# One fused attention and gating block on one core: start-up loads moved between two queues, idle matmuls added, a transpose issued a slot later, a last addition joined

## The chip, the core and the metric

The kernel runs on one core of a Trainium2 chip. The core has a matrix engine (TensorE, PE in the profile, with PEld for its weight loads), a vector engine (VectorE, DVE), an engine for functions (ScalarE, ACT), a general one (GpSimd, POOL) and an engine that here only issues transfers (SyncE, SP). Each has its own instruction queue, which it works through in order; they meet through semaphores. Transfers run on 16 DMA engines and are issued from SP's queue or from ACT's. The matrix engine writes to PSUM, in which this kernel keeps two double banks for scores (s_ps), two banks o_ps and two banks misc.

The metric is the device time of one execution in microseconds (us), less is better. The kernel before takes 1305.17 us, the median of three runs (1304.81 to 1305.69).

## The reference

```python
mod = (_silu(c) @ w_mod).reshape(c.shape[0], 6, 1, -1)
sa, ca, ga, sb, cb, gb = ...            # six rows of 512
h = _layernorm(x) * (1 + ca) + sa
x = x + ga * _A_ref(h, k_cache, v_cache, wq, wo)     # attention
h = _layernorm(x) * (1 + cb) + sb
x = x + gb * _B_ref(h, w_in, w_sp, b_sp, w_out)      # gated block
```

x has 2048 rows of 512. The attention has 32 query heads of 128, 8 heads of k and v with 2048 cached rows each, four query heads to one of k and v, softmax without a mask. The gated block projects to 2 x 896, applies gelu, normalises the second half, multiplies it along the rows with a 2048 x 2048 matrix w_sp, adds a bias, multiplies with the first half and projects back to 512. Everything comes and goes as bfloat16; sums are float32.

## The kernel before

**Units and iterations.** Rows are worked in 16 tiles of 128 (index j). A unit u is one group of four heads on one tile: 8 x 16 = 128 units, u = 16 g + j. One iteration `it` of the main loop issues the scores and exps of unit `it` in eight slots, and between them, by tables of functions to call at (iteration, slot), all the other work: the product with v of an earlier unit (`pv`), the output projection of a still earlier one (`wo_proj`), the query projection of a later group (`set_fill`), loads and norms. The order of every engine's queue is the order in which this Python code issues instructions; nothing reorders it.

**Rows and columns.** Of three successive units two are "by rows": their scores have query rows on partitions, the exps go to a row buffer, and each of the four heads is turned by a DMA transpose (pT) that SP issues (`turn_rows`), at slots 2, 4, 6 and at slot 0 of the next iteration. Their product with v comes two or three iterations later. The third unit, and all from unit 122 on, are computed already turned.

**Start.** At the start `c_bf` is loaded on ACT's queue, and on SP's queue x's first tile, two pieces of the modulation weights `wmod_a` (768 and 256 KB), half of k for group 0, weights of the first queries, and so on (L701 to L763). DVE casts c (L772), takes statistics of x's first tile (L697, L698); POOL makes the reciprocal root (L678, L682); DVE normalises (L686); ACT and DVE make silu(c). PE meanwhile runs `warm(10)`, idle matmuls on zeros (L777), then transposes x's tile (L897), multiplies the modulation weights with silu(c) (`mod_first`, L866), transposes part of k (`k_turn`, L856), runs two more idle matmuls, and projects the first queries (`first_q`, L927). DVE's copy to `modc` (L904) and the modulated tile `hT` (L805, L911) stand between `mod_first` and `first_q`. The first scores are L1040, their exps L1047.

**Second norm.** When the last group's output projection of tile j is done (in iteration `it`), `ln2` puts three steps into the table: `first` (statistics, reciprocal root) at slot 2 or 0 of the next iteration, `second` (normalisation to xn, and the DMA transpose xnT on SP's queue, L1207) at slot 4, and `third` (modulation of the turned tile into hT on DVE, L1214) at slot 3 of the iteration after. This happens from iteration 117 on. Iterations 117, 119 and 120 are units by rows, so that there SP also issues transposes of heads at even slots.

**Tail.** The gated block follows. For the last row tile the two halves of the final projection are multiplied with gb_rows by DVE (L1661), then x is added, one half by POOL and the other by DVE (L1665), and ACT's queue writes the tile (L1671).

Of the kernel before, what the change touches and what calls it, by code (L numbers as in the profile page):

```python
# [10 lines left out]
BF16 = mybir.dt.bfloat16  # L11
FP32 = mybir.dt.float32
ACT = mybir.ActivationFunctionType
ALU = mybir.AluOpType
AX = mybir.AxisListType
P = 128
# [559 lines left out]
def kernel(  # L576
# [19 lines left out]
    nc = tc.nc  # L596
    _, S, D = A_x.shape
    _, HKV, SK, DH = A_k_cache.shape
    HQ = A_wq.shape[1] // DH
    REP = HQ // HKV  # L600
# [5 lines left out]
    NDT = D // P  # L606
# [19 lines left out]
    wmod_dram = w_mod.rearrange("(p dt) n -> p dt n", p=P)  # L626
    c_dram = c[0].rearrange("(p j) -> p j", p=P)
# [18 lines left out]
    x_sb = res.tile([P, NT, D], BF16, name="x_sb")  # L646
# [10 lines left out]
    wmod_a = res.tile([P, NDT, 2 * D], BF16, name="wmod_a")  # L657
# [11 lines left out]
    def bank(name):  # L669
        return psum.tile([P, 512], FP32, name=name)  # L670
# [4 lines left out]
    def rstd_of(mv, n, tag):  # L675

        ve = stat.tile([P, CT], FP32, name=f"ve_{tag}")
        nc.gpsimd.tensor_scalar(  # L678
            out=ve[:, :n], in0=mv[:, :, 1], scalar1=LN_EPS, scalar2=None, op0=ALU.add
        )  # L680
        rstd = stat.tile([P, CT], FP32, name=f"rstd_{tag}", bufs=4)
        nc.gpsimd.tensor_tensor(out=rstd[:, :n], in0=ve[:, :n], in1=mhalf[:, :n], op=ALU.pow)  # L682
        return rstd

    def normalise(dst, src, mv, rstd):
        nc.vector.tensor_scalar(  # L686
            out=dst,
            in0=src,
            scalar1=mv,
            scalar2=rstd,  # L690
            op0=ALU.subtract,
            op1=ALU.mult,
        )

    def ln_stats(mv, j, src):
        st = stat.tile([P, 1, nc.vector.BN_STATS_DIM], FP32, name="bnst")
        nc.vector.bn_stats(out=st[:, 0, :], in_=src)  # L697
        nc.vector.bn_aggr(out=mv[:, j, :], in_=st[:])  # L698


    c_bf = res.tile([P, NDT], BF16, name="c_bf")  # L701
    nc.scalar.dma_start(out=c_bf[:], in_=c_dram)
    nc.sync.dma_start(out=x_sb[:, 0, :], in_=x_dram[:, 0, :])
    for kts in (slice(0, NDT - 1), slice(NDT - 1, NDT)):
        nc.sync.dma_start(out=wmod_a[:, kts, :], in_=wmod_dram[:, kts, 0 : 2 * D])
    k_nat = early.tile([P, SK], BF16, name="kT")

    def load_k_nat(half):
# [58 lines left out]
    zeros = late.tile([P, REP, DH], BF16, name="onorm", bufs=3)  # L767
# [2 lines left out]
    nc.gpsimd.memset(mean_bf[:], 1.0 / P)  # L770
    c_f = res.tile([P, NDT], FP32, name="c_f")
    nc.vector.tensor_copy(out=c_f[:], in_=c_bf[:])  # L772
    def warm(n):

        w_ps = bank("o_ps")
        for k in range(n):
            nc.tensor.matmul(  # L777
                w_ps[:].rearrange("p (r d) -> p r d", r=REP),
                lhsT=zeros[:, 0, :],
                rhs=zeros[:],  # L780
                start=True,
                stop=True,
            )
# [80 lines left out]
    def mod_first(kt, mc_ps):  # L864
        for col in range(2 * NDT):
            nc.tensor.matmul(  # L866
                mc_ps[:, col : col + 1],
                lhsT=wmod_a[:, kt, col * P : (col + 1) * P],
                rhs=sc_bf[:, kt : kt + 1],
                start=(kt == 0 and col == 0),  # L870
                stop=(kt == NDT - 1 and col == 2 * NDT - 1),
            )
        if kt == 0:
            nc.tensor.matmul(
                mc_ps[:, NDT : 2 * NDT],
                lhsT=mean_bf[:],
                rhs=ones_bf[:, 0:NDT],
                start=False,
                stop=False,
            )  # L880
# [10 lines left out]
    nc.vector.tensor_copy(out=sc_bf[:], in_=sc[:])  # L891
    xns0 = ln1_norm(0, 1, rstd0)
    mc_ps = bank("misc")
    warm(10)
    x_ps = bank("misc")[:].bitcast(BF16)[:, 0:D]
    for dt in range(NDT):
        nc.tensor.transpose(  # L897
# [1 line left out]
        )  # L899
    xT0 = res.tile([P, D], BF16, name="xn1", bufs=4)  # L900
    nc.vector.tensor_copy(out=xT0[:], in_=x_ps)
    for kt in range(NDT):
        mod_first(kt, mc_ps)
    nc.vector.tensor_copy(out=modc[:, 0 : 2 * NDT], in_=mc_ps[:, 0 : 2 * NDT])  # L904
    k_copy = k_turn((0, 1, 2, 3))
    warm(2)
    hT_of(0)
    for dt in range(NDT):
        dst, src = hTs[0][:, dt, 0:P], xT0[:, dt * P : (dt + 1) * P]
        if dt == 1:  # L910
            nc.scalar.activation(  # L911
                out=dst,
                in_=src,
# [87 lines left out]
    def at(it, slot, fn):  # L1001
        later.setdefault((it, slot), []).append(fn)
# [191 lines left out]
    def ln2(it, j):  # L1194

        st = {}

        def first():
            if j < NT - CT:
                ln_stats(mv2, j, x_sb[:, j, :])  # L1200
            st["rstd"] = rstd_of(mv2[:, j : j + 1, :], 1, "ln2")

        def second():
            xn = res.tile([P, D], BF16, name="xn2", bufs=2)
            normalise(xn[:], x_sb[:, j, :], mv2[:, j, 0:1], st["rstd"][:, 0:1])
            st["xnT"] = res.tile([P, NDT, P], BF16, name="xnT2", bufs=2)
            nc.sync.dma_start_transpose(out=st["xnT"][:], in_=xn[:])  # L1207

        def third():
            ch, c0 = j // CT, (j % CT) * P  # L1210
            if ch not in h2Ts:
                h2Ts[ch] = res.tile([P, NDT, 512], BF16, name="hT", bufs=NCH)
            for dt in range(NDT):
                nc.vector.tensor_scalar(  # L1214
                    out=h2Ts[ch][:, dt, c0 : c0 + P],
                    in0=st["xnT"][:, dt, :],
                    scalar1=modc[:, 4 * NDT + dt : 4 * NDT + dt + 1],
                    scalar2=modc[:, 3 * NDT + dt : 3 * NDT + dt + 1],
                    op0=ALU.mult,
                    op1=ALU.add,  # L1220
                )

        at(it + 1, 0 if j >= NT - CT else 2, first)
        at(it + 1, 4, second)
        at(it + 2, 3, third)

    mod_b = {}
# [120 lines left out]
    for g in range(1, HKV):  # L1348
        it = (g - 1) * NT
# [106 lines left out]
    for it in range(NU + 6):  # L1456
# [10 lines left out]
        for i in range(NSLOT):  # L1467
# [14 lines left out]
            elif pvs:  # L1482
                n = NSLOT // 2
# [10 lines left out]
        for u in wos:  # L1494
            if u >= (HKV - 1) * NT:
                ln2(it, u % NT)
        if it == NU + 2:
            free_b.close()
            mlp = fast.enter_context(tc.tile_pool(name="mlp", bufs=1, side="right"))
# [16 lines left out]
    for f in range(NFT):  # L1516
# [6 lines left out]
        out=ok1[:], in0=rall[:], scalar1=1.0 / SAFE, scalar2=None, op0=ALU.is_ge  # L1523
# [8 lines left out]
        out=bad[:], in0=okm[:], scalar1=-1.0, scalar2=1.0, op0=ALU.mult, op1=ALU.add  # L1532
# [99 lines left out]
    halves = [slice(hf * D // 2, (hf + 1) * D // 2) for hf in range(2)]  # L1632
# [23 lines left out]
        o2_half(hf, f)  # L1656
    j_end = NT - 1
    tmp = mlp.tile([P, D], FP32, name="tmp", bufs=2)[:].bitcast(BF16)[:, 0:D]
    yout = mlp.tile([P, D], BF16, name="yout", bufs=2)
    for hf in range(2):  # L1660
        nc.vector.tensor_tensor(  # L1661
            out=tmp[:, halves[hf]], in0=o2_half_ps[hf], in1=gb_rows[:, halves[hf]], op=ALU.mult
        )
    for hf, engine in ((0, nc.gpsimd), (1, nc.vector)):
        engine.tensor_tensor(  # L1665
            out=yout[:, halves[hf]],
            in0=tmp[:, halves[hf]],
            in1=x_sb[:, j_end, halves[hf]],
            op=ALU.add,
        )  # L1670
    nc.scalar.dma_start(out=out_dram[:, j_end, :], in_=yout[:])  # L1671
    fast.close()

# [35 lines left out]
```

## Time and profile before

| | |
|---|---|
| median of three runs | 1305.17 us (1304.81 to 1305.69) |
| profiled execution | 1306.55 us |
| its span, first to last instruction | 1304.8 us |
| PE busy | 1296.2 us, 99% |
| ACT busy | 1112.7 us, 85% |
| DVE busy | 685.9 us, 53% |
| POOL busy | 59.6 us, 5% |
| mean granted clock of PE | 0.999 |
| moved by DMA | 211.19 MB, 162 GB/s |

The profile is of one execution. Times in it run from the span's start. A timeline line gives start, duration, engine, source line, operation, written and read tiles, how often, and in brackets the idle time before it with what ended it; neighbours of one kind are merged, and the durations of matmuls include about 0.17 us in which the next is already running. PEq, SPq and ACTq are sequencers: an SPq line is the time in which SP issued a transfer, not the transfer. A line of waits gives who waited for whom, the total in us, how often, and the longest. "issue" is time in which an engine waited for nothing that the profile shows. The granted clock is the share of full speed at which PE was allowed to run, 1.00 at most.

### The profile page before, as it was taken

What the parts mean: (1) busy time and instruction counts of PE and PEld (TensorE: products, weight loads), DVE (VectorE), ACT (ScalarE), POOL (GpSimd) and SP (SyncE); (2) the same over time, 40 slices, a digit from 0 to 9 for tenths busy, and PEclk for the clock granted to TensorE, in tenths of its full rate; (3) what the DMA queues carried; (4) which work ended last, traced back from release to release, by engine and by line L of the source; (5) the groups of instructions that cost most, each with busy time, mean ns of one, the idle gap of its engine ahead of it and who ended that gap; (6) DMA issues with size and microseconds to landing.
All of it is one profiled execution on the core that took longest, in us unless ns stands there. A gap on an engine that the chain in (4) does not pass through costs nothing.

```text
span 1304.8 us, 22724 instructions
## 1 busy us (share of the span) xinstructions
PE 1296.2 (99%) x8662; PEld 700.7 (54%) x8662; DVE 685.9 (53%) x1777; ACT 1112.7 (85%) x1683; POOL 59.6 (5%) x100
## 2 busy tenths in 40 slices
PE   9999999999999999999999999999999999999998
PEld 7655555555555555555555555555555556644445
DVE  6635445544554455445545554555455566784444
ACT  6999999999999999999999999999999998650000
POOL 2000000000000000000000000000000133410000
PEclk9999999999999999999999999999999999999999
DMA  7999999999999999999999999999999983254300
GB/s 183 195 191 188 159 185 189 186 169 193 186 185 172 186 170 189 185 175 186 187 180 182 188 189 182 170 194 172 181 189 166 171 146 90 49 137 98 81 21 31
DMA packets 774998, 211.19 MB, mean 162 GB/s; under 512 B 759264, under 2 KB 773216, under 8 KB 774880
## 3 DMA queue, kind: packets, MB, share of 16 engines
q1 hardware_dynamic: 772432, 207.55, 87.6%
q10 hardware_dynamic: 2448, 2.10, 0.5%
q8 instruction: 70, 1.15, 0.4%
q14 instruction: 48, 0.39, 0.1%
HBM read 21.37 MB, written 2.10 MB: 18 GB/s over the span
## 4 chain that ended last, share of the span: by engine, by line
PE 99%; DMA 0%; ACT 0%; DVE 0%; SPq 0%; issue 0%
PE o_ps L1091 21%; PE s_ps L1019 21%; PE o_ps L1112 14%; PE s_ps L1056 13%; PE misc L1169 8%; PE misc L955 8%; PE misc L1549 7%; PE s_ps L1373 2%; PE s_ps L1412 2%; PE o_ps L1582 1%; PE s_ps L1040 0%; DMA kT<-in_A_k_cache_dram 0%; PE s_ps L1582 0%; ACT pT L1047 0%; ACT pn L1026 0%; PE o_ps L838 0%
## 5 line engine op out<-in xcount | busy, mean ns | idle before, releaser
L1019 PE MATMUL s_ps<-kT,qT 128*128 128x512 bf16 x1248 | 371.4, 379 | 0.1
L1026 ACT ACTIVATE win_sb<-s_ps 128x1024 bf16<-128x1024 f32 x312 | 319.0, 1023 | 3.4 <-PE s_ps L1019 0.7
L1091 PE MATMUL o_ps<-pT,v 128*128 128x512 bf16 x944 | 280.3, 379 | 0.4 <-issue 0.4
L1162 DVE SCALAR_TENSOR_TENSOR xacc<-misc,rall,xacc 128x512 f32<-128x512 f32 x304 | 227.5, 748 | 69.8 <-PE misc L1169 63.2
L1056 PE MATMUL s_ps<-qT,kT 128*128 128x512 bf16 x768 | 228.5, 379 | 0.0
L1063 ACT ACTIVATE pT<-s_ps 128x1024 bf16<-128x1024 f32 x208 | 209.7, 1024 | 11.7 <-PE s_ps L1056 3.6
L1026 ACT ACTIVATE pn<-s_ps 128x1024 bf16<-128x1024 f32 x208 | 212.7, 1023 | 2.3 <-PE s_ps L1019 0.5
L1091 PEld LDWEIGHTS <-v 128*128 128x128 bf16 x1248 | 121.9, 98 | 148.0 <-issue 0.8
L1169 PE MATMUL misc<-wo_g,oT 128*128 128x512 bf16 x512 | 194.3, 379 | 0.1
L1063 ACT ACTIVATE wsp<-s_ps 128x1024 bf16<-128x1024 f32 x176 | 179.7, 1023 | 12.7 <-PE s_ps L1056 4.8
L955 PE MATMUL misc<-hT,wq_g 128*128 128x512 bf16 (+1 forms) x544 | 190.5, 365 | 0.0
L1019 PEld LDWEIGHTS <-qT 128*128 128x128 bf16 x1248 | 121.4, 98 | 109.5 <-issue 0.4
L966 DVE CAST qT<-misc 128x512 bf16<-128x512 f32 x127 | 87.3, 687 | 153.8 <-PE misc L955 153.8
L1112 PEld LDWEIGHTS <-pT 128*128 128x128 bf16 x1792 | 119.6, 98 | 48.8
L1080 DVE TENSOR_TENSOR tot<-rs 128x1 f32<-128x1 f32 x312 | 48.5, 156 | 171.2 <-ACT win_sb L1026 114.8
L1112 PE MATMUL o_ps<-v,pT 128*128 128x129 bf16 x1792 | 137.6, 220 | 0.0
L1056 PEld LDWEIGHTS <-kT 128*128 128x128 bf16 x768 | 74.0, 98 | 81.2 <-issue 1.1
L1112 PEld LDWEIGHTS <-wsp 128*128 128x128 bf16 x1408 | 94.2, 98 | 41.6
L1112 PE MATMUL o_ps<-v,wsp 128*128 128x129 bf16 x1408 | 108.6, 220 | 0.0
L1026 ACT ACTIVATE wmod_a<-s_ps 128x1024 bf16<-128x1024 f32 x104 | 106.3, 1023 | 0.6 <-PE s_ps L1019 0.4
L1549 PE MATMUL misc<-wsp,z 128*128 128x512 bf16 (+2 forms) x560 | 100.5, 337 | 0.0
L1091 PE MATMUL o_ps<-wsp,v 128*128 128x512 bf16 x304 | 90.5, 379 | 0.0
(116 smaller groups left out, 896.4 us busy)
## 6 DMA issues: line engine op xcount, KB each, us to landing
wo_g<-in_A_wo_dram SPq DMA_DIRECT2D x8, 512.0 KB, 4.6
wq_g<-in_A_wq_dram SPq DMA_DIRECT2D x7, 512.0 KB, 4.1
v<-in_A_v_cache_dram SPq DMA_DIRECT2D x7, 512.0 KB, 4.8
wsp<-in_w_mod_dram SPq DMA_DIRECT2D x1, 2048.0 KB, 9.0
out_dram<-yout ACTq DMA_DIRECT2D x16, 128.0 KB, 1.7
pT<-win_sb SPq DMA_TRANSPOSE x117, 5.0
win_sb<-in_B_w_in_dram SPq DMA_DIRECT2D x1, 1792.0 KB, 7.4
x_sb<-in_A_x_dram SPq DMA_DIRECT2D x3, 512.0 KB, 6.1
```

Of the source, the lines that this page charges most:

```text
L955: nc.tensor.matmul(ps[0][:, o0 : o0 + n], lhsT=wqs[g][:, dt, hh * DH : (hh + 1) * DH], rhs=hTs[ch][:, dt, c0 : c0 + n], start=(dt == 0), s ...
L966: nc.vector.tensor_copy(out=dst, in_=src)
L1019: nc.tensor.matmul(s_ps[:, c * 512 : (c + 1) * 512], lhsT=qTs[b][:, hh, jj * P : (jj + 1) * P], rhs=groups[g]["kT"][:, k0 : k0 + 512], sta ...
L1026: nc.scalar.activation(out=rows_of(u, hh)[:, half * HK : (half + 1) * HK], in_=s_ps[:], func=ACT.Exp, scale=inv_sqrt_dh, accum_out=rsums[u ...
L1056: nc.tensor.matmul(s_ps[:, h * 512 : (h + 1) * 512].rearrange("p (r q) -> p r q", r=REP), lhsT=groups[g]["kT"][:, kt * P : (kt + 1) * P], ...
L1063: nc.scalar.activation(out=pTs[u][:, 2 * i : 2 * i + 2, :], in_=s_ps[:].rearrange("p (k q) -> p k q", k=2), func=ACT.Exp, scale=inv_sqrt_dh,)
L1080: nc.vector.tensor_tensor(out=tot[:], in0=rs[:, 2 * hh : 2 * hh + 1], in1=rs[:, 2 * hh + 1 : 2 * hh + 2], op=ALU.add)
L1091: nc.tensor.matmul(o_pss[u][:], lhsT=groups[g]["v1"][:, kt, 0:DH], rhs=pTs[u][:, kt, :], start=(kt == 0), stop=(kt == NKT - 1),)
L1112: nc.tensor.matmul(o_ps[:, hh % 2, 0 : DH + 1], lhsT=pTs[u][:, kt, hh * P : (hh + 1) * P], rhs=groups[g]["v1"][:, kt, 0 : DH + 1], start=( ...
L1162: nc.vector.scalar_tensor_tensor(out=xa[:], in0=X_ps[:], scalar=scale, in1=xa[:], op0=ALU.mult, op1=ALU.add)
L1169: nc.tensor.matmul(ps[0][:], lhsT=oTs[u][:, hh, :], rhs=groups[g]["wo"][:, hh, :], start=(hh == 0 or each), stop=(hh == REP - 1 or each),)
L1549: nc.tensor.matmul(g_pss[f][:, :n], lhsT=z2[:, st, f * P : (f + 1) * P], rhs=wsp[t][:, st, c0 : c0 + n], start=(st == 0), stop=(st == NT - ...
```

## The change

- c and the larger piece of the modulation weights change places: the weights' first three quarters are issued first on ACT's queue, c second on SP's queue behind x's first tile. The last quarter of the weights stays on SP's queue, third as before.
- `warm` takes a second argument, the number of 128-column blocks (4 unless given). `warm(10)` becomes `warm(13)`, and `warm(3, 1)`, three idle matmuls of 128 columns, is issued between the transposes of x's first tile and `mod_first`.
- In `ln2` the DMA transpose leaves `second` and becomes a step of its own, `turn`, at slot 5 instead of 4. Normalisation stays at slot 4 and `third` at slot 3 of the iteration after.
- The last tile's addition of x is one instruction on DVE over 512 columns; its result lies in a buffer of `gb`, the bias sum's tile of the gated block, and no longer in one of `yout`.

```diff
     c_bf = res.tile([P, NDT], BF16, name="c_bf")
-    nc.scalar.dma_start(out=c_bf[:], in_=c_dram)
+    nc.scalar.dma_start(
+        out=wmod_a[:, 0 : NDT - 1, :], in_=wmod_dram[:, 0 : NDT - 1, 0 : 2 * D]
+    )
     nc.sync.dma_start(out=x_sb[:, 0, :], in_=x_dram[:, 0, :])
-    for kts in (slice(0, NDT - 1), slice(NDT - 1, NDT)):
-        nc.sync.dma_start(out=wmod_a[:, kts, :], in_=wmod_dram[:, kts, 0 : 2 * D])
+    nc.sync.dma_start(out=c_bf[:], in_=c_dram)
+    nc.sync.dma_start(out=wmod_a[:, NDT - 1, :], in_=wmod_dram[:, NDT - 1, 0 : 2 * D])
...
-    def warm(n):
+    def warm(n, r=REP):
 
         w_ps = bank("o_ps")
         for k in range(n):
             nc.tensor.matmul(
-                w_ps[:].rearrange("p (r d) -> p r d", r=REP),
+                w_ps[:, 0 : r * DH].rearrange("p (r d) -> p r d", r=r),
                 lhsT=zeros[:, 0, :],
-                rhs=zeros[:],
+                rhs=zeros[:, 0:r, :],
                 start=True,
                 stop=True,
             )
...
-    warm(10)
+    warm(13)
...
     nc.vector.tensor_copy(out=xT0[:], in_=x_ps)
+    warm(3, 1)
     for kt in range(NDT):
         mod_first(kt, mc_ps)
...
             normalise(xn[:], x_sb[:, j, :], mv2[:, j, 0:1], st["rstd"][:, 0:1])
+            st["xn"] = xn
+
+        def turn():
             st["xnT"] = res.tile([P, NDT, P], BF16, name="xnT2", bufs=2)
-            nc.sync.dma_start_transpose(out=st["xnT"][:], in_=xn[:])
+            nc.sync.dma_start_transpose(out=st["xnT"][:], in_=st["xn"][:])
...
         at(it + 1, 4, second)
+        at(it + 1, 5, turn)
         at(it + 2, 3, third)
...
-    yout = mlp.tile([P, D], BF16, name="yout", bufs=2)
+    yout = mlp.tile([P, 512], BF16, name="gb", bufs=2)
...
-    for hf, engine in ((0, nc.gpsimd), (1, nc.vector)):
-        engine.tensor_tensor(
-            out=yout[:, halves[hf]],
-            in0=tmp[:, halves[hf]],
-            in1=x_sb[:, j_end, halves[hf]],
-            op=ALU.add,
-        )
+    nc.vector.tensor_tensor(out=yout[:], in0=tmp[:], in1=x_sb[:, j_end, :], op=ALU.add)
```

## The prediction

> **What bounds the kernel now.** I read the page's busy shares and the chain that ended last, then TensorE's (PE's) waits, then the timelines of the few places where it waits. Busy share and chain:
>
> ```profile
> PE 1296.2 (99%) x8662; PEld 700.7 (54%) x8662; DVE 685.9 (53%) x1777; ACT 1112.7 (85%) x1683; POOL 59.6 (5%) x100
> PE 99%; DMA 0%; ACT 0%; DVE 0%; SPq 0%; issue 0%
> ```
>
> PE is busy for 1296.2 of 1304.8 us and carries 99% of the chain. So 8.6 us of idle time, and the time in which PE runs slower than it could, are all that this change can touch. All of PE's waits in the span are these (waiting tile and line, releaser, total, times, longest):
>
> ```profile
> PE o_ps L777 <- DVE onorm L768: 1.2, 1, 1.2
> PE misc L897 <- DVE xn L686: 0.6, 1, 0.6
> PE s_ps L1040 <- ACT pT L1047: 0.5, 2, 0.3
> PE misc L866 <- DMA wmod_a<-in_w_mod_dram: 0.4, 1, 0.4
> PE o_ps L1091 <- issue: 0.4, 1, 0.4
> ```
>
> Four lie in the first 14 us, one in the last group of heads; the rest is the tail after the last matmul. The start in order of time (start, duration, engine, line, operation):
>
> ```profile
> 0.73 0.40 ACTq L702 DMA_DIRECT2D c_bf<-in_c_dram  x1
> 1.18 3.72 PE L777 MATMUL o_ps<-onorm 128*128 128x512 bf16 x10 [1.18 <-DVE onorm L768]
> 2.92 0.17 DVE L772 CAST c_f<-c_bf 128x4 f32<-128x4 bf16 x1 [1.66 <-DMA c_bf<-in_c_dram]
> 3.09 0.69 DVE L697 BATCH_NORM_STATS2 bnst<-x_sb 128x6 f32<-128x512 bf16 x1
> 5.49 0.40 PE L897 MATMUL misc<-ident,xn 128*128 128x128 bf16 x4 [0.59 <-DVE xn L686]
> 6.29 0.35 PE L866 MATMUL misc<-sc_bf,wmod_a 128*128 128x1 bf16 x8 [0.41 <-DMA wmod_a<-in_w_mod_dram]
> 7.42 0.17 DVE L904 COPY modc<-misc 128x8 f32<-128x8 f32 x1 [1.07 <-PE misc L866]
> 8.68 1.06 PE L927 MATMUL misc<-hT,wq_g 128*128 128x128 bf16 x8
> ```
>
> Two chains meet at 6.29: x's normalisation, which has run behind the cast of c on VectorE (DVE), and the weights' landing, for which PE waits 0.41. The windows of the start (length, busy times, then the granted clock, DMA share, GB/s):
>
> ```profile
> 4.00:7.40 3.40, 2.38 (x41) 1.38 (x39) 1.40 (x6) 0.00 (x0) 0.81 (x2) 1.00 1.06 353
> 7.40:10.80 3.40, 3.34 (x22) 2.44 (x23) 1.68 (x6) 0.86 (x2) 0.48 (x1) 0.51 1.21 255
> ```
>
> After a thin stretch the clock is at half for 3.4 us, over the first projection and the first scores. Then the one wait in the middle, on the queue of SyncE (SP) and on PE:
>
> ```profile
> 1048.41 1.19 SPq L1207 DMA_TRANSPOSE xnT<-xn  x1
> 1049.70 1.34 SPq L1076 DMA_TRANSPOSE pT<-pn  x1
> 1055.27 2.94 SPq L1076 DMA_TRANSPOSE pT<-win_sb  x1
> 1060.11 0.35 issue
> 1061.04 1.95 SPq L1207 DMA_TRANSPOSE xnT<-xn  x1
> ```
>
> The page's releaser is only "issue", but the transpose issued at 1055.27 is the fourth head of unit 119, takes about 5.1 to land (1060.4), and PE's next matmul, at 1060.46, is that unit's first product with v. That unit's second head (1049.70) stood behind xnT, whose input DVE finished at 1048.38.
>
> **The change, part by part.**
>
> *c behind x.* SP's issues are 0.46 apart (0.73, 1.19), so c is issued 0.46 later. Its 2.2 us to landing came beside x's 128 KB; now it flies beside 768 KB of weights on another queue. The nearest row for two busy queues is the output's: 1.7 us alone, median 2.4 and at most 2.8 while SP's transposes ran. So c is later by another 0 to 1.1; I take 0.3, since c is only 1 KB: cast at 3.68. The cast is DVE's first instruction after its memsets, and x's statistics, POOL's reciprocal root and the normalisation queue behind it: transposes at 6.25 instead of 5.49. ACT's exponential and sc wait with it, with room (4.67 now).
>
> *Weights first on ACT's queue.* They start 0.46 sooner, so land at 5.83 instead of 6.29 and PE's wait of 0.41 goes. ACT's table load waits for 0.40 of issue as it does now for c's. SP's queue loses a 0.44 issue and gains c's 0.40: later loads move by under 0.1. What is late next is x's chain: transposes at 6.25, four at 0.056 each (16 such matmuls in 0.89 in the tail, L1549) is 0.22, three small idle ones 0.17, so the modulation's matmuls begin at 6.64 and not 6.29: +0.35. Bounds: c not later at all gives 5.49+0.39 = 5.88, −0.41; c at its upper bound gives 7.44, +1.15. [...]
>
> *More idle matmuls.* The last three of thirteen run at full clock, 0.215 each: 0.65, ending at 5.55, before the transposes' input; hidden (if c is not late, they cost 0.06). Their effect is on the clock. PE streams in 4.0 to 7.4: idle matmuls 0.90, transposes 0.22, 33 one- to four-column matmuls almost nothing: about 1.1 of 3.4, and the clock fell. The change adds 0.82: 1.9 of 3.4. The stretch that raised the clock (1.18 to about 4) was 2.8 of 3.4. The threshold is somewhere between 1.1 and 2.8; 1.9 is near the middle, so the outcome is open. Held, first_q starts when hT is ready: modc at 7.77, hT 0.80 later (7.42 to 8.22 now), 8.57; eight matmuls 0.62, ACT's copy 0.41, four scores 0.60 and 0.07 of gaps: first exp at 10.27 instead of 11.14, −0.87. Dropped, everything is 0.35 late, +0.35. ACT runs its exps almost without a gap from there, so either carries through. Where the half-rate stretch begins is not set by anything in the kernel, so several executions mix both: I take the mean, −0.26. Whole range of the start: −1.24 (held, c not late, then bound by first_q's weights, landed at 8.2) to +1.15. [...]
>
> *The turn a slot later.* Sixteen xnT transposes, 1.19 to 1.95 on SP each, 2.4 to 3.8 to landing. They pass something only where a row unit issues a pT transpose at slot 4: iterations 117, 119 and 120. Elsewhere (spatial weights at even slots, oT at slot 0) SP's order stays. In 119 the second head goes out when its exp is done, about 1047.4, not 1049.70; heads three and four wait for exps and SP, and I take 1 us earlier for the fourth (0 to 2.3): more than 0.35, so PE's wait goes: −0.35. In 117 and 120 the price is that xnT goes out behind 1.9 us of pT issue, while its reader on DVE stays at slot 3 of the next iteration. From 117 there are 2.4 us of room (landed 1035.5, read 1037.92). From 120 there is none: issued 1061.04, landed 1064.54, read 1064.56. It is issued about 0.4 later (SP is a microsecond ahead by then), and DVE waits 0.4. Behind that wait stand the cast of qT, xn and the xacc sum; its sum ended at 1067.1 and PE needs the bank at 1067.58: 0.46 of room, nothing lost. Bounds: −0.35, and +1.5 with xnT a whole 1.95 later: DVE starts at 1066.5, the sum ends 2.56 behind that (as now, 1064.56 to 1067.12), at 1069.06, against 1067.58.
>
> *Last addition in one.* Now POOL and DVE each take a half, DVE's 1300.27 to 1300.85 (0.58 beside POOL's 0.67). A whole 512-column addition of that kind takes 0.42 (L1595). End at 1300.69: −0.16 (0 if it too took 0.58). Its tile now comes from gb's buffers, last read by DVE itself at 1290.8: no wait.
>
> **Sum**, against the profiled execution (1306.55, of which 1304.8 is span): −0.26 − 0.35 − 0.16 = −0.77, so 1305.8. The median of the runs shown, 1305.17, is 1.38 below that execution; on that scale 1304.4.
>
> **Rivals.**
> - *The clock holds throughout.* Start −0.87 to −1.24, rest as above: −1.4 to −1.75, 1303.4 to 1303.8. For it: streaming goes from 1.1 to 1.9 of 3.4. Against: x's chain is later, so the gap before the transposes grows (5.55 to 6.25).
> - *The change does not do what it says.* The clock falls as before and the fourth head lands no sooner, since the DMA share is 9 in tenths nearly everywhere: +0.35 + 0 − 0.16, 1305.4.
> - *xnT comes late.* In iteration 120 it lands 1.95 later, DVE stands, and PE loses up to 1.5 at 1067.6: −0.26 + 1.5 − 0.16 = +1.1, 1306.3.
> - *c is held up by the weights*, the slower side. If c takes as long as the weights themselves (5.1 to landing), it lands at 6.3, the modulation starts at 9.26, +2.97, and PE idles so long that the clock falls anyway: +2.97 − 0.35 − 0.16 = +2.46, 1307.6. It decides from c's landing at about 3.85 on: there +0.51 at the start eats the other two terms. For it: c's 128 packets start with those of the weights. Against: c lost nothing beside x, and outputs lost 0.7.
>
> **How the numbers follow.** The forecast 1304.4 has 0.46; the clock held 0.20; no effect 0.15; xnT late 0.07; c held up 0.12, mostly by less than its full price. Low end: 1303.4 less 0.4, the distance of the lowest run from the median, 1303.0. High end: start +1.15 and nothing gained elsewhere, 1306.3. The likeliest case alone spans 1303.8 to 1305.2. About 0.2% (2.6 us) is what a measurement of this kernel tells from no change, and no sum above reaches it, except that c's rival nearly does: faster 0.04, same 0.90, slower 0.06.
>
> **What would show it.** c_f's cast near 3.7, no wait of L866 for the weights, transposes near 6.3; the granted clock in 7.4 to 10.8 above 0.51 where the idle matmuls work; PE's wait near 1060 gone; DVE's wait for xnT at 1064 of a few tenths; one last addition of about 0.42. I am wrong if c lands after 4.5, if a new PE wait of over a microsecond stands near 1038 or 1065, or if the clock is at half for two stretches.

## The result, and the profile after

The changed kernel takes 1309.05 us (median of 9 runs, 1308.16 to 1309.45) beside 1305.42 for the kernel before on the same chip (9 runs, 1304.81 to 1306.38): 1.0027 times as long, 95% interval 1.0018 to 1.0035. It is slower by 3.6 us; the forecast was 1304.4 within 1303.0 to 1306.3. The profiled execution took 1309.01 us, of which 1307.2 is span.

Busy shares on the page after:

```profile
PE 1288.7 (99%) x8515; PEld 701.3 (54%) x8668; DVE 685.9 (52%) x1777; ACT 1112.8 (85%) x1683; POOL 59.1 (5%) x99
PE 97%; DMA 1%; issue 1%; ACT 1%; DVE 1%; POOL 0%; SPq 0%; ACTq 0%
```

PE's busy time can't be compared with the figure of before, because some 150 of its records are missing in this trace. The chain can: a DMA, ACT and DVE have come into it with 1% each. PE's longest waits after (waiting tile and line, releaser, total, times, longest; two of 0.2 in all are left out):

```profile
PE misc L899 <- DVE xn L686: 2.1, 1, 2.1
PE o_ps L779 <- DVE onorm L770: 1.2, 1, 1.2
PE misc L1172 <- DVE qT L969: 0.9, 2, 0.5
PE s_ps L1043 <- ACT pT L1050: 0.5, 2, 0.3
```

The wait for x's normalisation has grown from 0.6 to 2.1, the wait for the weights is gone, the wait near 1060 is gone, and a new one on qT has come, twice. The chain at the start, in order of time (start, duration, what), and then three lines of the timeline around it:

```profile
1.19 4.50 DMA c_bf<-in_c_dram
5.72 0.17 DVE c_f L774
5.89 0.61 DVE bnst L697
...
8.19 0.41 PE misc L899 x4
```

```profile
1.18 4.87 PE L779 MATMUL o_ps<-onorm 128*128 128x512 bf16 x13 [1.18 <-DVE onorm L770]
5.72 0.17 DVE L774 CAST c_f<-c_bf 128x4 f32<-128x4 bf16 x1 [4.46 <-DMA c_bf<-in_c_dram]
13.02 1.02 ACT L1050 ACTIVATE pT<-s_ps 128x1024 bf16<-128x1024 f32 x1 [0.68 <-PE s_ps L1043]
```

c, one kilobyte, takes 4.50 us from its issue to its landing. DVE stands 4.46 us in front of the cast, x's statistics follow at once (x itself, issued at 0.73, had landed 2.2 us later), and the first exponential comes at 13.02 instead of 11.14. The granted clock after, in the windows of the forecast and one more (length, busy times, clock, DMA share, GB/s):

```profile
4.00:7.40 3.40, 2.04 (x7) 0.62 (x5) 1.51 (x7) 0.20 (x1) 0.53 (x2) 1.00 0.99 327
7.40:10.80 3.40, 2.46 (x45) 2.13 (x47) 1.79 (x6) 0.49 (x1) 0.76 (x2) 0.65 1.00 255
10.80:14.20 3.40, 2.89 (x29) 2.55 (x29) 1.64 (x5) 1.55 (x3) 0.57 (x2) 0.84 1.03 229
```

The clock still falls: it reads 1.00 from 8.0 to 8.4 and 0.50 from 8.5 to 11.8, so the half-rate stretch begins a little behind the 2.1 us of idle time before the transposes, which start at 8.19. In the middle, the chain of iteration 118:

```profile
1037.30 4.57 DMA xnT<-xn
...
1041.89 0.98 DVE hT L1220 x4
1042.87 0.61 DVE qT L969
...
1043.52 0.38 PE misc L1172
```

xnT takes 4.57 to land, DVE's third step waits for it, qT's cast stands behind that step, and PE waits 0.53 for qT. In the tail one addition of 0.43 has taken the place of the two halves, and the store is issued 0.46 after the addition begins, instead of 0.66:

```profile
1302.84 0.43 DVE L1671 TENSOR_TENSOR gb<-tmp,x_sb 128x512 bf16<-128x512 bf16 x1
1303.30 0.34 ACTq L1672 DMA_DIRECT2D out_dram<-gb  x1
```

Where the time went can be read from instructions of POOL that every kernel here has in the same order: its clearing of v at 35.54 us in the profile of before, and its additions on line 1185 at 1024.78, 1059.62 and 1077.55 there. The time between such marks, in us, one profiled execution of each kernel (the runs are explained below):

| kernel | clearing of v at | to 1024.78's | with iteration 118 (to 1059.62's) | with 120 and 121 (to 1077.55's) | span |
|---|---|---|---|---|---|
| before | 35.54 | 989.24 | 34.84 | 17.93 | 1304.8 |
| before, again | 34.36 | 989.25 | 34.84 | 17.92 | 1303.5 |
| changed | 37.43 | 989.24 | 35.53 | 17.92 | 1307.2 |
| load order alone | 37.62 | 989.24 | 34.84 | 17.76 | 1306.7 |
| idle matmuls alone | 34.59 | 989.24 | 34.84 | 17.70 | 1303.5 |
| later turn alone | 34.37 | 989.24 | 34.84 | 18.08 | 1304.0 |
| both of these | 34.19 | 989.25 | 35.55 | 18.01 | 1304.1 |

All of the change lies in the first 37 us, in the stretch with iteration 118 and in the tail. Against the profiled execution of before it is +1.89, +0.69, 0 and about −0.2, together the +2.4 of the spans.

### The profile page after: what moved, and what is told of

Same layout as the page of the kernel before. It is cut to its first block, busy times and chain, and to the rows that moved or that the text cites. A ratio compares the mean times of both kernels' runs of the same rounds, so it can differ in the third digit from the quotient of the medians.

```text
span 1307.2 us, 22574 instructions
## 1 busy us (share of the span) xinstructions
PE 1288.7 (99%) x8515; PEld 701.3 (54%) x8668; DVE 685.9 (52%) x1777; ACT 1112.8 (85%) x1683; POOL 59.1 (5%) x99
## 4 chain that ended last, share of the span: by engine, by line
PE 97%; DMA 1%; issue 1%; ACT 1%; DVE 1%; POOL 0%; SPq 0%; ACTq 0%
PE s_ps L1022 20%; PE o_ps L1094 20%; PE o_ps L1115 14%; PE s_ps L1059 13%; PE misc L1172 8%; PE misc L958 8%; PE misc L1556 7%; PE s_ps L1380 2%; PE s_ps L1419 2%; PE o_ps L1589 1%; DMA xnT<-xn 1%; PE s_ps L1043 0%; DMA c_bf<-in_c_dram 0%; PE s_ps L1589 0%; ACT pT L1050 0%
## 5 line engine op out<-in xcount | busy, mean ns | idle before, releaser
L1022 PE MATMUL s_ps<-kT,qT 128*128 128x512 bf16 x1219 | 365.2, 379 | 2.3
L1094 PE MATMUL o_ps<-pT,v 128*128 128x512 bf16 x909 | 272.8, 379 | 1.3
L1172 PE MATMUL misc<-wo_g,oT 128*128 128x512 bf16 x479 | 181.8, 380 | 1.9 <-DVE qT L969 0.9
L958 PE MATMUL misc<-hT,wq_g 128*128 128x512 bf16 (+1 forms) x515 | 179.8, 364 | 0.5
```

The lines of the kernel that those rows point to most:

```text
L958: nc.tensor.matmul(ps[0][:, o0 : o0 + n], lhsT=wqs[g][:, dt, hh * DH : (hh + 1) * DH], rhs=hTs[ch][:, dt, c0 : c0 + n], start=(dt == 0), s ...
L1022: nc.tensor.matmul(s_ps[:, c * 512 : (c + 1) * 512], lhsT=qTs[b][:, hh, jj * P : (jj + 1) * P], rhs=groups[g]["kT"][:, k0 : k0 + 512], sta ...
L1094: nc.tensor.matmul(o_pss[u][:], lhsT=groups[g]["v1"][:, kt, 0:DH], rhs=pTs[u][:, kt, :], start=(kt == 0), stop=(kt == NKT - 1),)
L1172: nc.tensor.matmul(ps[0][:], lhsT=oTs[u][:, hh, :], rhs=groups[g]["wo"][:, hh, :], start=(hh == 0 or each), stop=(hh == REP - 1 or each),)
```

## Experiments

### The kernel before again, and the load order alone

`before_again` is the kernel before with nothing changed; `order_only` is the kernel before with this part of the diff only:

```diff
-    nc.scalar.dma_start(out=c_bf[:], in_=c_dram)
+    nc.scalar.dma_start(
+        out=wmod_a[:, 0 : NDT - 1, :], in_=wmod_dram[:, 0 : NDT - 1, 0 : 2 * D]
+    )
     nc.sync.dma_start(out=x_sb[:, 0, :], in_=x_dram[:, 0, :])
-    for kts in (slice(0, NDT - 1), slice(NDT - 1, NDT)):
-        nc.sync.dma_start(out=wmod_a[:, kts, :], in_=wmod_dram[:, kts, 0 : 2 * D])
+    nc.sync.dma_start(out=c_bf[:], in_=c_dram)
+    nc.sync.dma_start(out=wmod_a[:, NDT - 1, :], in_=wmod_dram[:, NDT - 1, 0 : 2 * D])
```

> The kernel before, unchanged. Its profiled execution took 1306.55 us, 1.1 more than the median of its runs. Theory: the place of PE's half-rate stretch differs between executions, and in most of them it costs less than in that profile; this profile then shows a half-rate stretch at another place than 7.4 to 10.8 us, or none, and a span nearer 1303.7 us. Rival: the stretch lies at the same place, and the 1.1 us are elsewhere. The ratio itself should be 1.000 within 0.1%.

> Only the loads' order is changed: the weights' three quarters first on ACT's queue, c behind x on SP's. Theory (c is held up by the weights, and the cast of c holds x's chain on DVE): c takes about 4.5 us to landing instead of 2.2, the first exp starts about 1.9 us later than in the profile of before, and the time rises by 2 to 3.2 us. Rival (the idle matmuls or the turn cost the time): within 0.5 us of before.

Measured: before again 1305.17 (11 runs, 1304.77 to 1306.44), ratio 0.9997 [0.9988, 1.0006]. Load order alone 1308.46 (11 runs, 1307.87 to 1309.34), ratio 1.0022 [1.0013, 1.0031], the larger part of the change's loss. The windows of the second profile of the kernel before:

```profile
4.00:7.40 3.40, 3.40 (x46) 1.97 (x45) 1.82 (x9) 0.12 (x1) 0.86 (x3) 1.00 1.07 359
7.40:10.80 3.40, 2.29 (x24) 1.49 (x23) 2.10 (x6) 2.10 (x4) 0.44 (x2) 1.00 1.20 278
```

Here the clock holds, in the very program whose first profile had it at 0.51 from 7.4 to 10.8. So the half-rate stretch is not in every execution; the first profile, span 1304.8, shows one that has it. How often it comes can't be counted from the times. Of 124 runs of the kernel before in four sets, 23 took 1306.0 us or more, the rest 1304.6 to 1305.9. But 14 of these 23 list a mean granted clock of 1.000, and 3.4 us at half rate in 1305 would make it 0.999, as in the first profile. So most of the slower runs are slow for another reason, which no run here shows. What the clock gives is in part lost again at once, since the second projection then comes to a weight that isn't there:

```profile
PE misc L927 <- DMA wq_g<-in_A_wq_dram: 0.9, 1, 0.9
```

Against this execution the start of the changed kernel is 3.07 later, not 1.89. With 0.69 in the stretch with iteration 118 and 0.05 less behind the last mark that is 3.7, the difference of the two spans; the medians differ by 3.6.

### What holds c back

Three load orders on the kernel before, each shown against the changed order. `c_before_x` lets c go ahead of x on SP:

```diff
+    nc.sync.dma_start(out=c_bf[:], in_=c_dram)
     nc.sync.dma_start(out=x_sb[:, 0, :], in_=x_dram[:, 0, :])
-    nc.sync.dma_start(out=c_bf[:], in_=c_dram)
```

`all_on_sp` moves the three quarters of the weights to SP, behind x and c:

```diff
-    nc.scalar.dma_start(
-        out=wmod_a[:, 0 : NDT - 1, :], in_=wmod_dram[:, 0 : NDT - 1, 0 : 2 * D]
-    )
     nc.sync.dma_start(out=x_sb[:, 0, :], in_=x_dram[:, 0, :])
     nc.sync.dma_start(out=c_bf[:], in_=c_dram)
+    nc.sync.dma_start(
+        out=wmod_a[:, 0 : NDT - 1, :], in_=wmod_dram[:, 0 : NDT - 1, 0 : 2 * D]
+    )
```

`quarter_first` puts only the first quarter (256 KB) on ACT, and the other three behind c on SP:

```diff
-        out=wmod_a[:, 0 : NDT - 1, :], in_=wmod_dram[:, 0 : NDT - 1, 0 : 2 * D]
+        out=wmod_a[:, 0:1, :], in_=wmod_dram[:, 0:1, 0 : 2 * D]
...
-    nc.sync.dma_start(out=wmod_a[:, NDT - 1, :], in_=wmod_dram[:, NDT - 1, 0 : 2 * D])
+    nc.sync.dma_start(out=wmod_a[:, 1:NDT, :], in_=wmod_dram[:, 1:NDT, 0 : 2 * D])
```

> The kernel before with the weights' three quarters first on ACT's queue, and on SP's queue c first and x behind it (c and x change places against the change). Theory (whatever is issued on the other queue after the 768 KB of weights is served only when most of them are through): c lands in about 2.2 us and its cast starts near 3, but now x, issued 0.46 later, lands near 5.5 us, so the first exp is as late as with the change and the time is 2.5 to 3.2 us over before. Rival (c's 128 packets of 8 bytes are slow beside any bulk load, wherever they stand): c's cast again after 5 us. Second rival (only c's place behind x matters): c near 3, x near 3.5, time within 0.5 us of before.

> The kernel before with x, c, and both pieces of the weights in this order on SP's queue, nothing on ACT's. c is issued 0.46 us later than before, as in the change, but ahead of the weights. Theory: c lands 2.2 to 2.5 us after its issue, at about 3.5, x's chain is 0.5 us later and hides most of it behind the weights, which are 0.4 later: +0.1 to +0.7 us. Rival (c behind x is what costs): +2.5 us or more.

> The kernel before with the change's load order, but only the first quarter of the modulation weights (256 KB) goes first on ACT's queue; the other three quarters go third on SP's queue, behind x and c. Theory, c stands behind the bytes that ACT's queue put into the shared transfer engines ahead of it: 768 KB cost c 2.3 us more than the 2.2 us it takes beside x, so 256 KB cost 0.8; c's cast at about 4.3 us, transposes of x at 6.8, no idle clock, and about 0.7 us on the kernel before: 1306.1. Rival, any bulk load issued on the other queue holds c back by a fixed time, whatever its size: cast at 5.7 us as in the changed kernel, time 1308.4.

| order | ahead of c | c's cast | x's statistics | first transposes | clearing of v at | median, us | ratio to before |
|---|---|---|---|---|---|---|---|
| before again | – | 3.14 | behind it | 5.62 | 34.36 | 1305.17 | 0.9997 [0.9988, 1.0006] |
| all_on_sp | x | 3.09 | 3.17 | 5.57 | 34.73 | 1306.37 | 1.0007 [0.9998, 1.0016] |
| quarter_first | x, 256 KB on ACT | 4.42 | 4.50 | 6.90 | 36.17 | 1307.70 | 1.0018 [1.0009, 1.0027] |
| changed | x, 768 KB on ACT | 5.72 | 5.80 | 8.19 | 37.43 | 1309.05 | 1.0027 [1.0018, 1.0035] |
| c_before_x | 768 KB beside it | 2.87 | 6.07 | 8.47 | 37.65 | 1308.75 | 1.0026 [1.0016, 1.0035] |

It is nothing in c itself. When c goes first it lands in 2.1 us, and x, one issue (0.46) behind, takes 4.9: the same time is lost, and DVE waits for x instead. With all loads on one queue, in order, neither is late. The time of `all_on_sp` is nevertheless 1.0 above before, where 0.1 to 0.7 was expected. The size test fits the theory of bytes ahead: 4.3 was expected with 256 KB, 4.42 came; a fixed price would have given 5.7. But the time was 1307.7, not the 1306.1 expected: behind 1.4 us of waiting before the transposes the clock fell (0.68 and 0.50 in the windows 8 to 10 and 10 to 12), and I had priced the delay without that.

The packet counts show whose packets moved. By queue (q1 is SP's, q10 ACT's): kind, packets, MB, share of the 16 engines. The changed kernel from 2.5 to 3.9, when c has been on SP's queue since 1.19 and the last quarter of the weights since 1.64:

```profile
q10 hardware_dynamic: 219, 0.45, 98.7%
q1 hardware_dynamic: 5, 0.00, 0.5%
```

The five are the last of x, none is c's. `c_before_x` from 2.8 to 4.4, with x issued at 1.19, and then the first instruction behind x's landing:

```profile
q10 hardware_dynamic: 280, 0.57, 99.6%
q1 hardware_dynamic: 1, 0.00, 0.2%
```

```profile
6.07 0.69 DVE L697 BATCH_NORM_STATS2 bnst<-x_sb 128x6 f32<-128x512 bf16 x1 [3.02 <-DMA x_sb<-in_A_x_dram]
```

ACT's queue has the engines almost to itself there. In the changed kernel some 345 of the 384 packets of its 768 KB had begun by 4.46, when c's first packet moved on SP's. One queue does not always shut out the other: in `quarter_first`, from 2.5 to 3.4, x (issued on SP at the same moment as the 256 KB on ACT, and with some of c's packets behind it) shares the engines with them:

```profile
q10 hardware_dynamic: 92, 0.17, 51.0%
q1 hardware_dynamic: 165, 0.12, 48.6%
```

Sharing has its price too: x took 3.5 us there, against 2.2 in the changed kernel (issue, size, us to landing):

```profile
x_sb<-in_A_x_dram SPq DMA_DIRECT2D x1, 128.0 KB, 3.5
```

The reading that fits all five orders is that each of the 16 engines finishes its whole share of one load before it takes up another queue's. It is an estimate: 768 KB went in 384 packets of 2 KB, evenly spread 24 for an engine, but the records don't name the engine of a packet, so the step to single engines is inferred. What was measured is that a load issued at the same moment as a large one got in ahead of it (beside 768 KB, x 2.2 us to landing and c 2.1) or shared the engines with it (x beside 256 KB, 3.5), and that one issued half a microsecond behind 768 KB landed 4.5 us (c) and 4.9 us (x) after its issue.

### The idle matmuls, and weights on ACT behind c

`warm_only` is the kernel before with the change's idle matmuls. `c_then_w_warm_tail` has them too, with the single last addition, and this order: c first and the three quarters second on ACT, x first and the last quarter second on SP.

```diff
-    warm(10)
+    warm(13)
...
+    warm(3, 1)
```

and against the changed order, in `c_then_w_warm_tail`:

```diff
+    nc.scalar.dma_start(out=c_bf[:], in_=c_dram)
     nc.scalar.dma_start(
         out=wmod_a[:, 0 : NDT - 1, :], in_=wmod_dram[:, 0 : NDT - 1, 0 : 2 * D]
     )
     nc.sync.dma_start(out=x_sb[:, 0, :], in_=x_dram[:, 0, :])
-    nc.sync.dma_start(out=c_bf[:], in_=c_dram)
```

> The kernel before with thirteen instead of ten idle matmuls and three small ones after the transposes, nothing else. Theory (they keep the clock up in the third of the executions in which it falls, and cost nothing where it holds): the slow third of the runs (near 1306.3) goes, median -0.1 to -0.5 us. Rival (they are what makes the change with the old load order 1.2 us slower): +0.5 us or more, and the profile shows where PE waits for them.

> c first on ACT's queue and the first three quarters of the weights behind it there, x first on SP's, the idle matmuls and the single last addition of the change, without the later turn. Theory, weights on ACT's queue do no harm when c and x are issued ahead of them: c's cast at 2.9 us as before, clock mostly held, tail 0.2 us shorter: 1305.0, and 1304.9 to 1305.9 in nearly all executions. Rival, weights on a second queue delay x or the later loads of SP's queue: start 0.5 us or more later, 1305.7 or above.

Measured: idle matmuls alone 1305.20 (11 runs, 1304.89 to 1305.92), 0.9998 [0.9989, 1.0007]; c then weights on ACT 1305.56 (11 runs, 1305.16 to 1306.04), 1.0001 [0.9992, 1.001]. So weights on ACT's queue do no harm once c and x are ahead of them (cast at 3.02); they do no good either. The 13 idle matmuls are not the fixed 0.65 us that I had counted. Idle matmuls and window from 4 to 6, `warm_only` and then `c_then_w_warm_tail`:

```profile
1.18 4.54 PE L777 MATMUL o_ps<-onorm 128*128 128x512 bf16 x13 [1.18 <-DVE onorm L768]
4.00:6.00 2.00, 2.00 (x14) 1.01 (x12) 0.98 (x6) 0.00 (x0) 0.81 (x2) 1.00 1.02 354
```

```profile
1.18 5.48 PE L779 MATMUL o_ps<-onorm 128*128 128x512 bf16 x13 [1.18 <-DVE onorm L770]
4.00:6.00 2.00, 2.00 (x6) 0.76 (x5) 0.98 (x5) 0.00 (x0) 0.81 (x2) 1.00 1.04 392
```

They ran at 0.43 each until PE sped up, and the moment of that differed between executions: 14 instructions in the one window, 6 in the other, though the clock reads 1.00 in both. The trace's record of the clock begins only where PE speeds up, at 4.37 in the one and 6.28 in the other, and the view takes the time ahead of it as 1.00. In the profiles here the 13 end between 5.50 and 6.78, and the transposes' input is there at about 5.5. In `c_then_w_warm_tail` PE begins the transposes at 6.50 behind them, 0.9 later than before again. In the changed kernel this costs nothing, since its transposes wait for c anyway.

Did they hold the clock? It held in all five profiles with them and the old order, or with c ahead; but it also held in five of the six with ten idle matmuls alone and neither c nor x held back, and in one of the two below with tiny ones behind the ten. `warm_only` has no run of 1306 or more among 11, where before has about one in five, but most of those are not the clock's (above). So whether they work is open; what is shown is that the median does not move.

### The later turn

`turn_only` is the kernel before with the new `turn` step; `warm_turn` adds the idle matmuls; `order_undone` is the whole change with the old load order, and `order_undone_again` the same kernel in another set of runs.

```diff
-            nc.sync.dma_start_transpose(out=st["xnT"][:], in_=xn[:])
+            st["xn"] = xn
+
+        def turn():
+            st["xnT"] = res.tile([P, NDT, P], BF16, name="xnT2", bufs=2)
+            nc.sync.dma_start_transpose(out=st["xnT"][:], in_=st["xn"][:])
...
+        at(it + 1, 5, turn)
```

> Only the second norm's turn a slot later. Theory: PE's wait of 0.35 us for the fourth head of unit 119 goes, but DVE waits about 2 us for xnT in iterations 118 and 121 and PE some 0.5 and 0.35 us for a bank behind it: +0.5 to +0.9 us in all. Rival (the slot is harmless, as the prediction had it): -0.35 us. Second rival (the turn is the main cost): +2 us or more.

> The whole change, but with the loads in the old order. Theory: the first exp is no later than before, so the time is within -0.5 to +0.7 us of before (the turn costs 0.7, the tail gives 0.2, the idle matmuls give 0 to 0.9). Rival (idle matmuls or turn are what costs): still 2 us or more slower.

> The kernel before with the additional idle matmuls and the later turn, old load order, old last addition. The two cost nothing each alone, but together with the new last addition they came to 1306.59. Theory, the idle matmuls start ACT and PE a few tenths of a us earlier, and the later turn then loses to the spatial weights' transposes in iteration 118: 1306.3 to 1306.8, with a wait of about 2 us for xnT near 1038 us. Rival, the last addition's tile is what moves something: 1305.2 and no such wait.

> The change with the old load order once more, to see another execution of it: 9 of its 11 executions took 1306.4 to 1306.7, its profiled one 1305.9. Theory, the slower ones lose in iteration 121 as well (a second PE wait on qT of about 0.5 to 0.7 us near 1070 us): 1306.6. Rival, they have the half-rate stretch at the start: the granted clock between 6 and 14 us falls to about 0.5 in one window, and PE's waits in the middle are as in the first look.

Measured: turn alone 1305.40 (0.9998 [0.9989, 1.0007]); with idle matmuls 1306.54 (1.0010 [1.0001, 1.0019]); order undone 1306.59 and, in the other set, 1306.37 (1.0008 [0.9999, 1.0017] and 1.0007 [0.9998, 1.0016]). The turn alone was expected to cost 0.5 to 0.9; in its profile the wait of DVE in iteration 121 came (1.97, and 0.51 on PE behind it), the one in 118 did not. The last addition is not in the loss: `warm_turn` keeps the old one. The second profile of the order undone has the turn's losses of the first, 35.70 and 18.01 in the columns of the first table (with iteration 118, with 120 and 121) against 35.63 and 18.08. It is later at the start, 34.75 against 34.09, though the clock held in both: its 13 idle matmuls end at 6.78 instead of 5.50. So neither theory of that expectation holds; these two profiles differ by the idle matmuls' own end.

Two parts that cost nothing alone cost 1.1 us together, 0.7 to 0.9 of it in the stretch with iteration 118. What differs there is xnT's landing. `turn_only`, xnT's issue on SP and its reader:

```profile
1034.27 1.47 SPq L1210 DMA_TRANSPOSE xnT<-xn  x1
...
1037.00 0.98 DVE L1217 TENSOR_SCALAR hT<-xnT,modc 128x128 bf16<-128x128 bf16 x4 [0.17 <-DMA xnT<-xn]
```

`warm_turn`, the chain there:

```profile
1034.01 4.64 DMA xnT<-xn
1038.65 0.02 issue
1038.67 0.98 DVE hT L1218 x4
```

2.7 against 4.64, with the same transfers ahead of it. The difference is one packet that isn't the program's data. In `warm_turn` a load of program code begins at 1036.59; in `turn_only` at 1037.86, when xnT has landed (queue, packets, MB, share of 16 engines, from 1036.5 to 1036.6 and from 1037.8 to 1037.9):

```profile
q8 instruction: 1, 0.02, 55.3%
```

```profile
q8 instruction: 1, 0.02, 60.3%
```

The packet records of `warm_turn` there (start in us, time taken in ns, bytes). xnT's data are followed by 32 packets of 4 bytes; 28 of them are done by 1036.40:

```
1036.487     7       4
1036.503     7       4
1036.587   876   16384   code
1037.391   947     256
...
1037.449    25       4
1037.462    18       4
...
1037.713   626     256
```

The last two come 0.95 us behind the others, as the 16 KB come to their end (1037.46), and xnT counts as landed only at 1038.65, some 0.3 after the slow 256-byte packets of the next transpose that began at 1037.39 to 1037.71 have ended (1038.36). That the landing waited for these too is inferred from that order alone.

Two kernels tell whether it is the code load or the idle matmuls' time. They have the later turn, the old ten idle matmuls, and behind them six or eighteen of one column, which make PE's program as much longer as the change does (or three times as much) and take 0.29 and 0.59 us, ahead of the transposes.

```diff
     def warm(n):
...
+        for k in range(6 if n > 2 else 0):
+            nc.tensor.matmul(
+                w_ps[:, 0:1],
+                lhsT=zeros[:, 0, :],
+                rhs=zeros[:, 0, 0:1],
+                start=True,
+                stop=True,
+            )
```

> The later turn alone, with six idle matmuls of one column more at the start: they take next to no time, but PE's program is six matmuls longer, as it is in the change. Theory, the 16 KB loads of program code move with PE's instruction count; the later turn alone is clear of the one in iteration 118 by 3.5 us from xnT's issue, and with six matmuls more it comes 2.5 us behind it, on one of the 16 transfer engines, so that xnT lands 4.6 instead of 2.7 us after its issue: a wait of about 2 us on DVE near 1038 us, one of 0.6 on PE behind it, 1306.1. Rival, the idle matmuls' own time (a start some tenths earlier or later) brings the transposes of iteration 118 together: no such wait here, 1305.4.

> The same with eighteen idle matmuls of one column. Theory, the code load moves by three times as much, to about 1 us behind xnT's issue, ahead of the end of its data: xnT is held up little or not at all, 1305.3 to 1305.7, while the transposes ahead of it on SP's queue may land later. Rival, anything that moves the code load earlier keeps the wait: 1306.1 again.

| kernel | code load after xnT's issue | xnT lands after | stretch with iteration 118 | median, us |
|---|---|---|---|---|
| turn alone | 3.6 | 2.7 | 34.84 | 1305.40 |
| turn, 6 tiny | 2.7 | 4.81 | 35.67 | 1306.31 |
| turn, 18 tiny | 1.5 | 4.21 | 35.25 | 1306.31 |
| turn, idle matmuls | 2.6 | 4.64 | 35.55 | 1306.54 |
| changed | 2.5 | 4.57 | 35.53 | 1309.05 |

Six tiny matmuls bring the whole loss: `turn_six_tiny` 1306.31 (11 runs, 1306.06 to 1308.29), 1.0009 [1.0, 1.0018], where 1306.1 was expected; in the chain of its profile:

```profile
1035.88 4.81 DMA xnT<-xn
```

That profiled execution, 1308.29, is the slowest of the 11: it has a half-rate stretch at the start as well (0.59 from 7.4 to 10.8), which leaves the stretch with iteration 118 as it is. Eighteen were expected to clear it and don't: the code load then falls into xnT's data and still holds it (4.21). So the load need not hit the last packets; 1.5 to 2.8 us behind the issue it held xnT in all six profiles in which it fell there, `order_undone` and its repeat included. With eighteen the loss in that stretch is only 0.41; 0.24 more than with the turn alone comes in 120 and 121 (18.32 against 18.08), and the rest of the difference of the medians isn't explained. Nor does the count of instructions alone fix the load's place: counted from the clearing of v, six more bring it 1.0 earlier with the later turn (1002.4 and 1002.5 against 1003.5), but only 0.3 in `warm_only` (1003.2).

### The reader a slot later

`third_later` is the later turn with `third` at slot 4 instead of 3; `third_later_tail` adds the single last addition. Both keep the old loads and the ten idle matmuls.

```diff
         at(it + 1, 4, second)
+        at(it + 1, 5, turn)
-        at(it + 2, 3, third)
+        at(it + 2, 4, third)
```

> The kernel before with the turn at slot 5 and its reader on DVE at slot 4 instead of 3. Theory (behind the later turn DVE stands at slot 3 and PE then waits for a bank): the waits of DVE for xnT in iterations 118 and 121 shrink to under 0.7 us, PE's waits for qT's cast and for the fourth head are both gone, and the time is 0.2 to 0.6 us below before. Rival (the reader's slot does not matter): as with the turn alone, within 0.2 us of before.

> The kernel before with the later turn, its reader on DVE a slot later too, and the single last addition; old load order, old number of idle matmuls. Theory, the turn gives nothing, the addition 0.2 us: 1305.1. Rival, the reader's later slot pays for the stall in iteration 121 as well: 1304.7.

Measured: 1305.28 (0.9997 [0.9988, 1.0006]) and 1304.90 (11 runs, 1304.34 to 1305.80; 0.9997 [0.9988, 1.0006]; before in that set 1305.36). With the reader later, the stretch over iterations 120 and 121 falls from 17.92 to 17.41: this is the gain that the later turn had promised, and with `third` at slot 3 the wait for xnT gives it back. `third_later_tail` has the lowest median of all, but its interval takes in no change, so it isn't shown to beat the kernel before.

## Why the prediction was wrong

**c behind x: the step that failed.** I took c's time on the way as 2.2 plus 0.3, at most 1.1 more, from the output's rows (1.7 alone, 2.4 to 2.8 beside transposes). It was 4.50, and the cast came at 5.72 instead of the 3.68 of the forecast. Those rows were a poor neighbour: there a store met transposes in packets of 256 bytes, here c came half a microsecond behind 384 packets of 2 KB. The rival "c is held up by the weights" had the mechanism; its landing of 6.3 was too late (5.69 measured) and its time of 1307.6 still too low, since it was reckoned against a profile whose clock had fallen already. I gave it 0.12 because c lost nothing beside x. But x and c were issued at the same moment, and `c_before_x` shows that half a microsecond is what matters. The clock then fell, as that rival had it: it fell in all four profiles in which c or x was held back, and in two of the other thirteen. That the idle wait is the reason is inferred from that.

**Weights first on ACT.** PE's wait of 0.41 for them went, as predicted, and was worth nothing with x's chain 2 us later. With c first on ACT and the weights behind it the start comes out no sooner than before.

**The clock and the scale.** The idle matmuls did not prevent the half-rate stretch in the changed kernel, where PE stood idle for 2.1 us before the transposes. The threshold between 1.1 and 2.8 of 3.4 us of streaming was an estimate from one profile, and no run shows one: `third_later_tail` held its clock with PE busy for 1.35 of the 2 us from 4 to 6, and the first profile, whose clock fell, had 1.29 there. A second error is one of scale, about 0.6 us: I read the first profile as typical and carried its sum over by the 1.38 between that execution and the median, while the −0.87 for a held clock was counted as a gain. That profile has the half-rate stretch; the second one, at 1305.32 close to the median, already has the clock held. With the clock held on both sides the forecast's own terms would have been +0.35 at the start, −0.35 and −0.16, 1305.0.

**Idle matmuls "hidden", at most 0.06.** Wrong in the other kernels, where they end up to 1.2 us later than the 5.55 I had; right in this one, behind c's wait.

**The turn.** The fourth head of unit 119 did go out sooner, and the wait of 0.35 near 1060 went. In iteration 120 I expected xnT 0.4 later, from 1.42 behind POOL's mark at 1059.62 to some 1.8. It went out 3.82 behind that mark (1066.02 against 1062.20 in the changed kernel), since a transpose of a row unit's head (issued at 1062.36) held SP for 3.57 just ahead of it:

```profile
1062.36 3.57 SPq L1079 DMA_TRANSPOSE pT<-wmod_a  x1
1066.02 1.22 SPq L1213 DMA_TRANSPOSE xnT<-xn  x1
1068.51 0.98 DVE L1220 TENSOR_SCALAR hT<-xnT,modc 128x128 bf16<-128x128 bf16 x4 [1.80 <-DMA xnT<-xn]
1070.14 0.38 PE L1172 MATMUL misc<-wo_g,oT 128*128 128x512 bf16 x1 [0.34 <-DVE qT L969]
```

DVE waited 1.8 and PE 0.34, which pays back the 0.35. In iteration 118 I had counted 2.4 us of room; xnT's landing took them all and PE lost 0.7. That a load of program code would hold a transfer was in none of my cases.

**The last addition.** −0.16 forecast; −0.20 from the addition's start to the store's issue (0.66 to 0.46). No run changes it alone, and behind the last mark the changed kernel is 0.05 to 0.17 shorter than the two profiles of before.

**The sum.** Against the second profile of before, which is close to the median: start +3.07, iteration 118 +0.69, 120 and 121 nothing, behind the last mark −0.05: +3.7, as the spans have it, where the medians differ by 3.6. The experiments leave little open: that an engine finishes its share of a load is inferred from counts of all 16 together, the +1.0 of `all_on_sp` is explained only in part, by 0.37 at the start of its profiled execution, and why the clock falls in some executions and not in others is open.

## What to carry to other kernels

The small load that a chain waited for was best issued before the large one here, on whichever queue: a second queue was no second path, and half a microsecond behind 768 KB cost 2.6 us (cast at 5.72 against 3.14). The same moment was not always soon enough: it cost c and x nothing beside 768 KB (2.1 and 2.2 us to landing), but x 1.3 us beside 256 KB (3.5). Before a sum is made against one profiled execution, ask whether that execution is like those that make the median; a second profile of the same program had another clock and another wait. The 2.4 us of slack on xnT's transfer were used up when a load of code fell into it (4.2 to 4.8 us to landing instead of 2.7), and six instructions added at the program's start moved where it fell (1.0 us earlier with the later turn).

## What the runs showed of the hardware

- A 16 KB load of program code took 0.88 us in one packet (`warm_turn`), and a transpose into whose time it fell landed 4.2 to 4.8 us after its issue instead of 2.7. Six one-column matmuls some 1,030 us earlier decided whether that happened.
- The moment at which PE went from 0.43 to about 0.22 us for a 512-column matmul at the program's start varied between executions: 13 of them ended anywhere between 5.50 and 6.78 us. A window's clock of 1.00 didn't show it (4 to 6 in `warm_only` and `c_then_w_warm_tail`, 14 and 6 instructions), since the record of the clock began at that moment, 4.37 and 6.28 there.
- In all six profiles in which the clock fell at the start, its record has the fall 3.41 us after that moment (4.03 and 7.44 in the first profile, 5.03 and 8.45 in the changed kernel's), and half rate for 3.41 us from there, 6.83 in `order_only`.
- Where both queues got a load at the same moment, the engines shared them (165 and 92 packets in 0.9 us, beside 256 KB), or the smaller went first (x beside 768 KB, 2.2 us). Behind 768 KB on the other queue, SP's queue got 5 and 1 packets in 1.4 and 1.6 us against 219 and 280.
